# A complex linear-attention chunk rewritten: scores from two 64-row products per head, a block-diagonal state, no regrouping copies, hardware scans, and one subtraction on GpSimd

## The chip, the cores and the metric

The kernel runs on one core of a Trainium2 chip, with its five engines (TensorE, here PE; VectorE, DVE; ScalarE, ACT; GpSimd, POOL; SyncE, SP). The metric is the device time of one execution in microseconds; the kernel before takes 1257.93 us (median of three runs, 1257.11 to 1259.96). The profile and its rows are of one further execution of 1253.42 us.

## The reference, cut to what matters

Three layers follow each other. The first is a complex linear recurrence for each of 4 x 8 heads with 48 values per head and 768 steps; the other two are a dense layer with an ELU and a top-2 mixture of 8 experts:

```
S_re, S_im = ar*S_re - ai*S_im + outer(k[t], v[t]),  ar*S_im + ai*S_re      # per head, 48 x 48
y[t] = q[t] @ S_re                                                          # only the real part is read
x = y as rows [3072, 384]
g = elu(x @ w_in);  x = g @ w_out                                           # 384 -> 2048 -> 384
logits = x @ w_gate + log1p(exp(x @ w_noise)) * noise;  top 2 of 8 experts
out += weight * (relu(x @ w1[e]) @ w2[e])                                   # 384 -> 1024 -> 384
```

In (ar, ai) each step's factor is scaled so that its size is at most 0.999. All inputs are float32, except w_in and w_out, which come as float64 and are decoded on the chip.

## The kernel before

The recurrence is computed in chunks of 128 steps. A unit u is one chunk of two of the four batches; there are 12 units, and within a unit the batch index i is 0 or 1. Heads are taken in pairs p (four pairs per batch); a pair fills 128 partitions with 64 each, of which 48 are used (the rest are padding). For every unit the kernel makes the running product of the factors' sizes (tile `E`), its angle as cosine and sine (tile `X`, index 0 and 1), and from them the scaled keys `KK` and queries `X`, each with a cosine part and a sine part. The score of query t and key s of one head is the sum over 48 channels of cos-part times cos-part plus sin-part times sin-part.

In the kernel before, TensorE computes this sum as one product over 128 rows per head: 64 rows hold the cosine part and 64 the sine part of the same head. What DVE computes stands otherwise, with the two heads of a pair in the two halves of the partitions, so `by_head` (lines 678 to 684) regroups it, with three copies of 64x512 for the keys and three for the queries of each (u, i): 144 copies in all. The state `St` also stands by pair, and `diag` (L770) regroups it into one tile `Sc` per i with four copies of 48x192. In `y` (lines 787 to 805) a head's output is the query times `Sc` plus the masked scores `P` times `v`; the 128 tokens are split into two halves of 64 columns of the array (`halves`).

`m_pieces` makes the running product in `E` with steps over strided slices: seven of 128x128 elements (L633), four of 128x64 (L639), and one of 128x840 (L644) per unit.

The dense layer takes the 256 tokens of one unit in eight steps s (`f_pieces`): `l1` multiplies into `ph`, ACT and DVE form the ELU in `ge`, ACT rounds it to the high part `gh` (L859), DVE subtracts to get the low part `gl` (L860), and `l2` of the step two later multiplies both into `y`. `ge`, `gh` and `gl` have two buffers each. `r_pieces` picks the experts and POOL writes their tables by indirect DMA (L967). The expert layer runs at the end, when all units are done, from about 760 us on.

The order of work on each engine is not that of the code: `arrange` collects all instructions, gives each a cost, groups some into runs that stay together, and lists them by priority and by when their inputs should be ready; the engines then work each through its own list in order. PSUM is held in two rings of two banks for the attention: the rings' string gives `sc0`, `sc1`, `upd` and `y` one ring, the transposes and angles the other.

Of the kernel before, what the change touches and what calls it, by code (L numbers as in the profile page):

```python
# [27 lines left out]
def arrange(tc):  # L28
# [58 lines left out]
    def cost(n):  # L87
        i, k, c = ins[n], kinds[n], cells[n]
        if eng[n] == "PE":
            if k != "Matmult":  # L90
                return 20, 20
            mv = i.ins[0]
            dt = str(mv.dtype)
            cols = math.prod(x[1] for x in mv.bass_ap.ap[1:])
            if "32r" in dt:
                return (8 + .4385 * cols if cols > 128 else 110), 170 + .4385 * cols
            if "bf" in dt:
                return 26, 166
            if i.is_transpose:
                return 110, 273  # L100
            if i.tile_size[1] != 128 or i.tile_size[0] != 128:
                return 72, 229
            return (223, 387) if cols <= 128 else (1.72 * cols, 1.72 * cols + 170)
# [11 lines left out]
        if eng[n] == "DVE":  # L115
            if k == "Memset":
                return 30 + c * .8, 60 + c * .8
            if k == "Reciprocal":
                return 60 + c * 6, 150 + c * 6
            r = 1.042  # L120
            if k == "TensorCopy" or k == "TensorScalarPtr" and sum(x[4] == 0 for x in acc[n]) == 1:
                if not psum_in[n]:
                    r = .53
            if k == "TensorTensor" and c <= 128 and any(getattr(o, "bass_ap", None) is not None and len(o.bass_ap.ap) > 1 and o.bass_ap.ap[-1][0] > 1 and o.bass_ap.ap[-1][1] > 1 for o in i.outs):
                r = 1.9
            s = 58 + c * r + (60 if k == "TensorScalarPtr" and scal[n] else 0)
            return s, s + 92
# [4 lines left out]
        if k == "Memset":  # L132
            return 100 + c * .55, 100 + c * .55
        return 25, 25
# [5 lines left out]
    for n, i in enumerate(ins):  # L140
        e = eng[n]
        p = prev.get(e)
        if e == "PE" and p is not None and kinds[n] == kinds[p] == "Matmult":
            a, b = acc[p][0], acc[n][0]
            same = a[0] == b[0]
# [49 lines left out]
    for key, ts in tag.items():  # L195
        ts.sort(key=lambda t: users[t][0])
        nb = tiles[ts[0]].bufs or tiles[ts[0]].tag_meta.bufs
        for k, t in enumerate(ts):
# [3 lines left out]
            if k and nb > 1:  # L202
                p = users[ts[k - 1]]
                mine = set(p)
                roots = [x for x in p if not (deps[x] & mine)]
# [145 lines left out]
def tile_kernel(ctx, tc, q, k, v, a_re, a_im, w_in, w_out, w_gate, w_noise, noise, w1, w2, qp, kp, vp, ap,  # L351
# [73 lines left out]
    Sc = []  # L425
    for b in range(NB):
        s = wa.tile([128, HP, 2, D], F32, name=f"Sc{b}", bufs=1)
        nc.gpsimd.memset(s, 0.0)
        Sc.append(s)
# [182 lines left out]
    def m_pieces(u):  # L612

        P = []
        R = 8
        NK = L // R

# [12 lines left out]
        def cm1(t):  # L630
            def f():
                x = ET[u].rearrange("p q (k r) -> p (q k) r", r=R)
                tt(x[:, :, t], x[:, :, t], x[:, :, t - 1], op=OP.mult)  # L633
            return f

        def cm2(h):
            def f():
                x = ET[u].rearrange("p q (a b r) -> p (q a) b r", r=R, b=2 * h)[:, :, :, R - 1]
                tt(x[:, :, h:], x[:, :, h:], x[:, :, h - 1:h].to_broadcast([128, NP * NK // (2 * h), h]), op=OP.mult)  # L639
            return f  # L640

        def cm3():
            x = ET[u].rearrange("p q (k r) -> p q k r", r=R)
            tt(x[:, :, 1:, :R - 1], x[:, :, 1:, :R - 1],  # L644
               x[:, :, :NK - 1, R - 1:R].to_broadcast([128, NP, NK - 1, R - 1]), op=OP.mult)
            nc.vector.tensor_reduce(guard[:, u, :, 3], ET[u][:, :, L - 1].rearrange("p (i h) -> p i h", i=NB),
                                    axis=AX.X, op=OP.min)
        for t in range(1, R):
            P.append((0.2, cm1(t)))
        h = 1  # L650
        while h < NK:
            P.append((0.2, cm2(h)))
            h *= 2
        P.append((1.0, cm3))
        return P

    def a_pieces(u):
# [20 lines left out]
        def by_head(x, t):  # L678


            copy = nc.vector.tensor_copy
            copy(t[:64], x[64:, 0])
            copy(x[64:, 0], x[:64, 1])
            copy(x[:64, 1], t[:64])

        def kk(i):
            def f():
# [5 lines left out]
                by_head(k, nat["k", u, i])  # L693
            return f

        def qq(i):
            def f():
# [4 lines left out]
                by_head(x[:, :, o], b[:, o])  # L702
# [10 lines left out]
    def b_pieces(u):  # L713
# [18 lines left out]
        def upd(i):  # L732
            def f():
# [3 lines left out]
                for p in range(HP):  # L737
                    for x in range(2):
                        for j in range(2):
                            mm(pu[64 * j:64 * j + 64, p, x, :], kts[j][:, p, 64 * x:64 * x + 64],  # L740
# [25 lines left out]
        def diag(i):  # L766
            def f():
                for j in range(2):
                    for x in range(2):
                        nc.vector.tensor_copy(Sc[i][64 * x:64 * x + D, :, j, :],  # L770
                                              St[bat(u, i)][64 * j:64 * j + D, :, x, :])
            return f

        def sc(i):
            def f():
                ps = [psa.tile([128, HP, L], F32, name=f"sc{j}", **ring(f"sc{j}")) for j in range(2)]
                for p in range(HP):
                    for j in range(2):
                        mm(ps[j][:, p, :], KK[u, i][:, j, p, :], X[u][:, j, i * HP + p, :],  # L779
                           start=True, stop=True)  # L780
# [6 lines left out]
        def y(i):  # L787
            def f():
                b = bat(u, i)
                py = psa.tile([128, Dm], F32, name="py", **ring("y"))  # L790
                for p in range(HP):
                    for j in range(2):
                        h = 2 * p + j
                        oh = slice(h * D, (h + 1) * D)
                        halves = [slice(z * (L // 2), (z + 1) * (L // 2)) for z in range(2)]
                        if c:
                            for z in halves:
                                mm(py[z, oh], X[u][:, j, i * HP + p, z], Sc[i][:, p, j, :], start=True, stop=False,
                                   skip_group_check=True)
# [36 lines left out]
    def f_pieces(u):  # L836
# [4 lines left out]
        def l1(s):  # L841
            def f():
# [9 lines left out]
                with sooner(PAR.get("fs", 0.0)):  # L852
# [7 lines left out]
                    tt(gl, e, gh.bitcast(F32), op=OP.subtract)  # L860
# [718 lines left out]
```

## Time and profile before

| | |
|---|---|
| median of the runs | 1257.93 us |
| profiled execution, its span | 1253.42 us, 1251.6 us |
| PE busy | 1160.8 us, 93% of the span |
| DVE busy | 786.7 us, 63% |
| ACT busy | 648.9 us, 52% |
| POOL busy | 234.4 us, 19% |
| TensorE's granted clock, mean | 0.972 |

Busy shares are means over the whole span; the stages differ. Up to about 136 us the dense layer's weights are decoded beside the first units of attention; from there to about 760 us attention and dense layer run interleaved; after that come the experts. A matmul's row carries a duration with its latency, and matmuls overlap, so the distance from one start to the next says what a matmul takes of PE.

### The profile page before, as it was taken

How to read it: one execution, taken by the hardware profiler on the slowest of the kernel's cores; microseconds unless marked ns; L12 is line 12 of the kernel's file. 1: busy time of each engine (PE TensorE's matmuls, PEld its weight loads, DVE VectorE, ACT ScalarE, POOL GpSimd, SP SyncE). 2: the span in 40 equal slices, each digit the busy share in tenths (PEclk: the TensorE clock that was granted, in tenths of full speed). 3: DMA queues.
4: the chain of work that ended last, by engine and by line, in shares of the span. 5: the costliest groups of instructions: out<-in, count | busy, mean ns of one | idle time of the engine just before them, and what ended most of it. 6: DMA issues, size and time to landing. Idle time of an engine off the chain costs nothing.

```text
span 1251.6 us, 22832 instructions
## 1 busy us (share of the span) xinstructions
PE 1160.8 (93%) x8821; PEld 1070.9 (86%) x8821; DVE 786.7 (63%) x1782; ACT 648.9 (52%) x1299; POOL 234.4 (19%) x265
## 2 busy tenths in 40 slices
PE   4786998999999999899999999799999999999997
PEld 2464988888998999899999898789898989898996
DVE  5798998987987979697863556344434343443322
ACT  6877876768776777576554464332323232332111
POOL 2111000002002000200200302432424242424222
PEclk9697999999999999899999999999999999999999
DMA  6345520220220202120100133343424242423111
GB/s 218 118 160 179 182 81 24 72 94 12 84 75 21 81 22 79 18 92 31 30 11 28 52 103 119 109 127 96 134 90 136 83 137 85 131 85 108 36 45 34
DMA packets 64309, 107.05 MB, mean 86 GB/s; under 512 B 19967, under 2 KB 46310, under 8 KB 64192
## 3 DMA queue, kind: packets, MB, share of 16 engines
q1 hardware_dynamic: 50096, 65.65, 16.9%
q0 software_dynamic: 14096, 39.86, 10.2%
q8 instruction: 71, 1.16, 0.4%
q14 instruction: 46, 0.38, 0.1%
HBM read 86.98 MB, written 20.70 MB: 86 GB/s over the span
## 4 chain that ended last, share of the span: by engine, by line
PE 51%; DVE 25%; issue 14%; ACT 6%; DMA 2%; POOL 2%; POOLq 0%; SPq 0%; DVEq 0%; ACTq 0%
PE mpo L1096 18%; PE mph L1074 17%; PE ph L850 4%; PE y L874 4%; DVE gl L860 2%; DVE ge L856 2%; DVE E L633 2%; DVE X L701 2%; PE mtp L1059 1%; DVE P L783 1%; DVE KK L692 1%; DVE Sc L770 1%; PE sc L779 1%; ACT L577 1%; POOL table L967 1%
## 5 line engine op out<-in xcount | busy, mean ns | idle before, releaser
L1076 ACT ACTIVATE egh<-mph 128x320 fp32r<-128x320 f32 (+1 forms) x128 | 66.3, 518 | 233.9 <-PE mpo L1096 141.7
L967 POOL DMA_INDIRECT table<-route x48 | 47.1, 981 | 593.4 <-DVE route L961 275.4
L1096 PE MATMUL mpo<-weh,egh 128*128 128x384 f32 (+1 forms) x448 | 151.6, 338 | 0.0
L1096 PE MATMUL mpo<-weh,egl 128*128 128x384 f32 (+1 forms) x448 | 151.6, 338 | 0.0
L1096 PE MATMUL mpo<-wel,egh 128*128 128x384 f32 (+1 forms) x448 | 151.2, 337 | 0.0
L874 PE MATMUL y<-woh,gh 128*128 128x400 f32 x384 | 138.9, 362 | 0.0
L1101 DVE SCALAR_TENSOR_TENSOR ac<-mpo,slots,ac 128x384 f32<-128x384 f32 (+1 forms) x49 | 30.2, 617 | 171.5 <-PE mpo L1096 171.5
L874 PE MATMUL y<-woh,gl 128*128 128x400 f32 x384 | 133.0, 346 | 3.1 <-DVE gl L860 3.1
L874 PE MATMUL y<-wol,gh 128*128 128x400 f32 x384 | 131.5, 342 | 0.0
L1077 DVE SCALAR_TENSOR_TENSOR egl<-mph,egh 128x320 fp32r<-128x320 f32 (+1 forms) x128 | 75.1, 587 | 80.2 <-ACT egh L1076 80.2
L850 PE MATMUL ph<-xh,wih 128*128 128x256 f32 x576 | 106.4, 294 | 8.1 <-DVE ge L856 8.1
L1027 ACT ACTIVATE weh<-raw 128x384 fp32r<-128x384 f32 x128 | 65.3, 522 | 84.2 <-PE mpo L1096 60.0
L850 PE MATMUL ph<-xl,wih 128*128 128x256 f32 x576 | 101.5, 285 | 0.0
L850 PE MATMUL ph<-xh,wil 128*128 128x256 f32 x576 | 101.4, 285 | 0.0
L1104 POOL DMA_INDIRECT out_dram<-ac,slots x56 | 55.2, 987 | 239.4 <-DVE ac L1101 216.4
L850 PEld LDWEIGHTS ph<-xh,wih 128*128 128x128 f32 x576 | 88.4, 193 | 12.0 <-DVE ge L856 7.5
L854 ACT ACTIVATE ge<-ph 128x512 f32<-128x512 f32 x96 | 57.2, 596 | 63.5 <-DVE gl L860 39.7
L859 ACT ACTIVATE gh<-ge 128x512 fp32r<-128x512 f32 x96 | 60.1, 628 | 54.8 <-PE y L874 51.8
L860 DVE TENSOR_TENSOR gl<-ge,gh 128x512 fp32r<-128x512 f32 x96 | 66.2, 690 | 34.9 <-ACT gh L859 34.2
L856 DVE SCALAR_TENSOR_TENSOR ge<-ge,ph 128x512 f32<-128x512 f32 x96 | 65.5, 683 | 33.6 <-ACT ge L855 32.3
L1028 DVE TENSOR_TENSOR wel<-raw,weh 128x384 fp32r<-128x384 f32 x128 | 69.3, 555 | 23.9 <-ACT weh L1027 22.1
L850 PEld LDWEIGHTS ph<-xh,wil 128*128 128x128 f32 x576 | 83.8, 193 | 0.0
(207 smaller groups left out, 2831.9 us busy)
## 6 DMA issues: line engine op xcount, KB each, us to landing
raw<-in_moe_w_dram SPq DMA_DIRECT2D x128, 192.0 KB, 2.6
nat_a<-in_a_rows_dram SPq DMA_DIRECT2D x24, 512.0 KB, 3.6
raw<-in_moe_w_in_dram POOLq DMA_DIRECT2D x16, 384.0 KB, 3.7
raw<-in_moe_w_out_dram POOLq DMA_DIRECT2D x16, 384.0 KB, 3.5
q<-in_q_pairs_dram SPq DMA_DIRECT2D x24, 256.0 KB, 3.7
k<-in_k_pairs_dram SPq DMA_DIRECT2D x24, 256.0 KB, 2.8
vt<-in_v_rows_dram SPq DMA_DIRECT2D x24, 192.0 KB, 2.7
out_dram<-zero SPq DMA_DIRECT2D x24, 192.0 KB, 4.5
```

The costliest lines, as they stand in the source:

```text
L850: mm(ph[:, j, :], w[:, z, :], x[:, z, :], start=n == 0, stop=n == 3 * KD - 1)
L856: stt(e, e, -1.0, ph, op0=OP.add, op1=OP.max)
L859: act(gh, e, AF.Copy)
L860: tt(gl, e, gh.bitcast(F32), op=OP.subtract)
L874: mm(d["y"][i], g[:, j, i * L:(i + 1) * L], w, start=s == 0 and j == 0 and n == 0, stop=s == NS - 1 and j == 1 and n == 2)
L967: st = nc.gpsimd.indirect_dma_start(out=table[:, :], out_offset=bass.IndirectOffsetOnAxis(ap=idx, axis=0), in_=row, in_offset=None)
L1027: act(w[0], raw, AF.Copy)
L1028: tt(w[1], raw, w[0].bitcast(F32), op=OP.subtract)
L1074: mm(ph[:, :n], w[:, z, :], x[:, z, :], start=k == 0, stop=k == 3 * KD - 1)
L1076: act(gs[0][:, f, :n], ph[:, :n], AF.Relu)
L1077: stt(gs[1][:, f, :n], ph[:, :n], 0.0, gs[0][:, f, :n].bitcast(F32), op0=OP.max, op1=OP.subtract)
L1096: mm(po[:m], x[:, f, o:o + m], w, start=k == 0, stop=k == 3 * FE - 1)
```

## The change

Six edits, all in the first two stages:

- The scores of a head are two products of 64 rows each (cosine part, then sine part) that add up in the same PSUM bank. The two heads of a pair use the two halves of the array's rows, alternately. `by_head` and its 144 copies are gone.
- The state is one tile `Sc` for both i, with the two heads of a pair block-diagonal: 128 rows by 96 columns for each pair and part. `diag` is two copies of 64x384. A product of query and state covers both heads: 96 columns instead of 48, and as many instructions as before.
- The update `upd` takes keys from the cosine or sine transpose instead of from the head's.
- The running product is a scan instruction for each of the 8 pairs of a unit (128x128), instead of 12 strided multiplications.
- `gl` is computed by GpSimd instead of DVE.
- The planner has costs for the new instructions, keeps matmuls of 64 rows together as one run, and ties a buffer's next tile to the first root of the previous one instead of all.

```diff
@@ arrange
+            if i.tile_size[1] == 128 and i.tile_size[0] == 64:
+                return 117, 330
...
+            if getattr(i, "is_tensor_tensor_scan", False):
+                return 58 + c * 2.084, 150 + c * 2.084
...
-            same = a[0] == b[0]
+            same = a[0] == b[0] or tuple(i.tile_size) == tuple(ins[p].tile_size) == (64, 128) and not i.is_transpose
...
-                roots = [x for x in p if not (deps[x] & mine)]
+                roots = [next(x for x in p if not (deps[x] & mine))]
@@ tile_kernel
+    Sc = wa.tile([128, HP, 2, 2 * D], F32, name="Sc", bufs=1)
+    nc.gpsimd.memset(Sc, 0.0)
@@ m_pieces
+        def cum(q):
+            def f():
+                x = ET[u][:, q]
+                nc.vector.tensor_tensor_scan(x, x, ones, 1.0, op0=OP.mult, op1=OP.mult)
+            return f
...
+        for q in range(NP):
+            P.append((0.4, cum(q)))
+        P.append((0.1, least))
@@ a_pieces
-                by_head(k, nat["k", u, i])
...
-                by_head(x[:, :, o], b[:, o])
@@ b_pieces
-                            mm(pu[64 * j:64 * j + 64, p, x, :], kts[j][:, p, 64 * x:64 * x + 64],
+                            mm(pu[64 * j:64 * j + 64, p, x, :], kts[x][:, p, 64 * j:64 * j + 64],
...
-                    for x in range(2):
-                        nc.vector.tensor_copy(Sc[i][64 * x:64 * x + D, :, j, :],
-                                              St[bat(u, i)][64 * j:64 * j + D, :, x, :])
+                    nc.vector.tensor_copy(Sc[64 * j:64 * j + 64, :, :, j * D:(j + 1) * D],
+                                          St[bat(u, i)][64 * j:64 * j + 64])
...
-                    for j in range(2):
-                        mm(ps[j][:, p, :], KK[u, i][:, j, p, :], X[u][:, j, i * HP + p, :],
-                           start=True, stop=True)
+                    for x in range(2):
+                        for j in range(2):
+                            h = slice(64 * j, 64 * j + 64)
+                            mm(ps[j][:, p, :], KK[u, i][h, x, p, :], X[u][h, x, i * HP + p, :],
+                               start=x == 0, stop=x == 1, skip_group_check=True)
...
+                    if c:
+                        for x in range(2):
+                            for z in halves:
+                                mm(py[z, 2 * p * D:(2 * p + 2) * D], X[u][:, x, i * HP + p, z], Sc[:, p, x, :],
+                                   start=x == 0, stop=False, skip_group_check=True)
@@ f_pieces
-                    tt(gl, e, gh.bitcast(F32), op=OP.subtract)
+                    nc.gpsimd.tensor_tensor(gl, e, gh.bitcast(F32), op=OP.subtract)
```

The order of instructions moves with it. On PE, this is one unit's scores and the start of its outputs before, in the middle of the program (`sc_5438` and `sc_5439` are the two heads' banks of one batch, numbers are buffers):

```order
L779 MATMUL sc_5438<-X,KK 128x128
L602 MATMUL tp<-tri,nat_a 128x128 x4
L779 MATMUL sc_5438<-X,KK 128x128 x3
L602 MATMUL tp<-tri,nat_a 128x128 x4
L779 MATMUL sc_5439<-X,KK 128x128 x4
L850 MATMUL ph<-xh,wih 128x256 x3
L850 MATMUL ph<-xl,wih 128x256 x3
L850 MATMUL ph<-xh,wil 128x256 x3
L624 MATMUL tp<-ident,nat_a 128x128 x4
L798 MATMUL py<-Sc_109,X 64x48 x2
L801 MATMUL py<-vt,P 64x48 x2
L798 MATMUL py<-Sc_109,X 64x48 x2
```

And this is the same place in the changed kernel, from the end of such a run of scores, of which two rows stand here:

```order
L759 MATMUL sc_4697<-X,KK 128x128
L759 MATMUL sc_4698<-X,KK 128x128
L626 MATMUL tp<-ident,nat_a 128x128 x8
L855 MATMUL y_3152<-woh,gh 128x400
L855 MATMUL y_3152<-wol,gh 128x400
L855 MATMUL y_3152<-woh,gl 128x400
L705 MATMUL tp<-ident,KK 128x128 x8
L855 MATMUL y_3153<-woh,gh 128x400
L855 MATMUL y_3153<-wol,gh 128x400
L855 MATMUL y_3153<-woh,gl 128x400
L776 MATMUL py<-Sc,X 64x96 x4
L782 MATMUL py<-vt,P 64x48 x4
```

The scores of a (u, i) were eight products, one bank after the other and split around other work; they are now 16 products that alternate between the two banks, in one piece. Over the whole program the pieces of PE's list in which the array is split into smaller tiles go from 43 to 64: 24 of them are the scores, and the outputs and updates make 40.

On DVE, this is a stretch from a middle unit before, where keys and queries of one batch are scaled and regrouped:

```order
L682 COPY k<-KK 64x512
L700 TENSOR_TENSOR E<-E,q 128x512
L683 COPY KK<-KK 64x512
L701 TENSOR_TENSOR X<-X,E 128x2x512
L860 TENSOR_TENSOR gl<-ge,gh 128x512 x2
L817 TENSOR_TENSOR xl<-tp,xh 128x3x128
L682 COPY E<-X 64x512
L684 COPY KK<-k 64x512
L683 COPY X<-X 64x512
L856 SCALAR_TENSOR_TENSOR ge<-ge,ph 128x512 x2
L817 TENSOR_TENSOR xl<-tp,xh 128x3x128
L684 COPY X<-E 64x512
```

And a stretch with the same steps of a middle unit in the changed kernel (the list prints the scans of L635 under another name):

```order
L672 TENSOR_TENSOR KK<-KK,k 128x512
L611 SCALAR_TENSOR_TENSOR X<-X,tp 128x512 x2
L673 TENSOR_TENSOR KK<-KK,X 128x1024
L763 TENSOR_TENSOR P<-sc_5397,causal 128x512
L763 TENSOR_TENSOR P<-sc_5398,causal 128x512
L739 TENSOR_TENSOR s_5060<-sx,al 128x384
L681 TENSOR_TENSOR X<-X,E 128x2x512
L635 SCALAR_TENSOR_TENSOR E<-E,ones 128x128 x4
L748 COPY Sc<-St_108 64x8x48 x2
L740 TENSOR_TENSOR sx<-sx,al 128x384
L635 SCALAR_TENSOR_TENSOR E<-E,ones 128x128
L741 TENSOR_TENSOR St_106<-sx,s_5060 128x4x48
```

## Rows read from the trace of the kernel before

**Rows 1.** Busy times by stretch; columns are named in the first line.

```profile
core 0: us, PE busy (x) PEld busy (x) DVE busy (x) ACT busy (x) POOL busy (x), PEclk, DMA share, GB/s
0.00:150.00 150.00, 108.22 (x681) 81.82 (x682) 123.00 (x281) 110.28 (x241) 22.14 (x46) 0.84 0.51 169
150.00:450.00 300.00, 280.21 (x2901) 266.35 (x2900) 267.15 (x630) 218.88 (x427) 16.22 (x16) 0.99 0.20 63
450.00:750.00 300.00, 285.92 (x2539) 276.81 (x2538) 204.40 (x474) 180.02 (x335) 31.40 (x38) 0.99 0.16 47
750.00:1251.00 501.00, 486.49 (x2707) 445.89 (x2705) 192.13 (x400) 139.72 (x300) 164.60 (x165) 0.99 0.32 98
```

**Rows 2.** Who PE waited for, 150 to 760 us: total us, times, longest.

```profile
PE ph L850 <- DVE ge L856: 8.1, 11, 2.1
PE pr L949 <- DVE route L944: 6.3, 3, 2.7
PE tp L602 <- ACT nat_a L581: 4.6, 2, 3.9
PE y L874 <- DVE gl L860: 3.1, 4, 0.9
PE mtp L1059 <- DMA xr<-xs,slots: 2.6, 2, 2.5
...
PE tp L815 <- DVE X L607: 0.2, 1, 0.2
```

**Rows 3.** Chain of waits, 150 to 450 us, shares of this stretch.

```profile
by line: issue 9.1%; PE y L874 7.6%; PE ph L850 7.1%; DVE gl L860 5.3%; DVE ge L856 4.9%; DVE E L633 4.3%; DVE Sc L770 3.4%; DVE X L701 3.3%; DVE P L783 3.0%; DVE KK L692 2.4%; ACT L577 2.1%; PE sc L779 2.0%; ACT X L578 1.8%; PE tp L602 1.7
```

**Rows 4.** DVE groups up to 760 us: busy us, mean ns, idle before.

```profile
L860 DVE TENSOR_TENSOR gl<-ge,gh 128x512 fp32r<-128x512 f32 x96 | 66.2, 690 | 34.9 <-ACT gh L859 34.2
L633 DVE TENSOR_TENSOR E<-E 128x128 f32<-128x128 f32 x84 | 34.3, 408 | 1.6 <-ACT E L625 1.1
L692 DVE TENSOR_TENSOR KK<-KK,X 128x1024 f32<-128x1024 f32 x24 | 29.2, 1219 | 25.3 <-ACT X L578 25.2
L770 DVE COPY Sc<-St 48x192 f32<-48x192 f32 x80 | 20.6, 258 | 1.3
L639 DVE TENSOR_TENSOR E<-E 128x64 f32<-128x64 f32 x48 | 13.5, 282 | 0.2
L644 DVE TENSOR_TENSOR E<-E 128x840 f32<-128x840 f32 x12 | 12.5, 1040 | 0.0
L683 DVE COPY KK<-KK 64x512 f32<-64x512 f32 x24 | 10.1, 421 | 0.7
L783 DVE TENSOR_TENSOR P<-sc,causal 128x512 f32<-128x512 f32 x48 | 32.8, 685 | 1.6 <-PE sc L779 1.6
```

**Rows 5.** PE in order of time: start us, us, then the instructions.

```profile
240.03 0.34 PE L874 MATMUL y<-wol,gh 128*128 128x400 f32 x1
240.21 0.34 PE L874 MATMUL y<-woh,gl 128*128 128x400 f32 x1
240.48 0.32 PE L798 MATMUL py<-Sc,X 128*64 128x48 f32 x4
...
242.27 0.29 PE L801 MATMUL py<-vt,P 128*64 128x48 f32 x4
242.48 0.45 PE L874 MATMUL y<-woh,gh 128*128 128x400 f32 x1
242.77 0.35 PE L874 MATMUL y<-wol,gh 128*128 128x400 f32 x1
...
268.08 1.16 PE L779 MATMUL sc<-X,KK 128*128 128x128 f32 x8 [0.94 <-DVE X L683]
268.99 0.43 PE L874 MATMUL y<-woh,gh 128*128 128x400 f32 x1
```

**Rows 6.** POOL and ACT: a memset's group, and who waited for gl.

```profile
L428 POOL MEMSET Sc<- 128x384 f32 x2 | 0.9, 437 | 0.0
  ACT ge L854: 39.7, 39
```

More of the change, by code (lines that the diff above doesn't have):

```diff
@@ L133, in cost @@
             return 100 + c * .55, 100 + c * .55
+        if k in ("TensorTensor", "TensorReduce"):
+            s = 160 + c * (2.1 if k == "TensorTensor" else 1.3)
+            return s, s + 40
         return 25, 25
@@ L424, in tile_kernel @@
         St.append(wa.tile([128, HP, 2, D], F32, name=f"St{b}", bufs=1))
[L425 to L429, printed above, removed]
+    Sc = wa.tile([128, HP, 2, 2 * D], F32, name="Sc", bufs=1)
+    nc.gpsimd.memset(Sc, 0.0)
     def bat(u, i):
@@ L614, in m_pieces @@
         P = []
-        R = 8
-        NK = L // R
         def size(i):
@@ L628, in m_pieces, with least @@
             P.append((0.5, size(i)))
-        def cm1(t):
+        def cum(q):
             def f():
-                x = ET[u].rearrange("p q (k r) -> p (q k) r", r=R)
-                tt(x[:, :, t], x[:, :, t], x[:, :, t - 1], op=OP.mult)
-            return f
[L636 to L645, printed above, removed]
+                x = ET[u][:, q]
+                nc.vector.tensor_tensor_scan(x, x, ones, 1.0, op0=OP.mult, op1=OP.mult)
+            return f
+        def least():
             nc.vector.tensor_reduce(guard[:, u, :, 3], ET[u][:, :, L - 1].rearrange("p (i h) -> p i h", i=NB),
                                     axis=AX.X, op=OP.min)
[L648 to L654, printed above, removed]
+        for q in range(NP):
+            P.append((0.4, cum(q)))
+        P.append((0.1, least))
         return P
@@ L676, in g1 @@
             return f
[L678 to L684, printed above, removed]
         def kk(i):
@@ L790, in f @@
                 py = psa.tile([128, Dm], F32, name="py", **ring("y"))
+                halves = [slice(z * (L // 2), (z + 1) * (L // 2)) for z in range(2)]
                 for p in range(HP):
+                    if c:
[3 more added lines that the diff above has]
+                                   start=x == 0, stop=False, skip_group_check=True)
                     for j in range(2):
@@ L794, in f @@
                         oh = slice(h * D, (h + 1) * D)
[L795 to L799, printed above, removed]
                         for z in halves:
```

## Prediction

> **What bounds the kernel now.** I read the busy times by stretch first [rows 1]. After 750 us the experts keep PE busy for 486.5 of 501 us, and no edit touches them: that stage only moves with its start. Everything is decided before. Up to 150 us PE works 108 us and DVE 123, with ACT close behind at 110: the weights' decoding and the first units keep DVE longest, and PE waits. From 150 to 750 us PE is busy 566 of 600 us, and DVE 267 of 300 us in the first half and 204 in the second. So two engines are nearly full there, and the question is which of them the other waits for.
>
> Who PE waited for says it [rows 2]: eleven rows from 8.1 down to 0.2 us, 33.6 us in all, and nine of them, 26.4 us, name DVE. That is no more than the idle 34 us of rows 1, so a change that only relieves DVE can give back about 34 us in this stretch and not more. The chain of waits for 150 to 450 us [rows 3] agrees: PE's two dense-layer lines lead it, but `gl` (5.3% of 300 us), `E` L633 (4.3%) and `Sc` (3.4%) stand on it with 39 us, all three lines that the change alters. That these 39 us lie on the chain doesn't make them a gain, since PE's own list is 93% full beside them.
>
> **What DVE loses.** Durations are from [rows 4]. Each of the six groups of regrouping copies has 24 instructions of 0.41 to 0.43 us (one group stands there); 144 of them are 60.5 us. `gl` is 96 x 0.690 = 66.2 us. The running products are 34.3 + 13.5 + 12.5 = 60.3 us; in their place come 96 scans. No scan is in the trace: at least 0.28 us (the 64-element multiplication, half as many elements), at most 0.69 us (a 512-element one). I take 0.41 us, the row with as many elements, so 39 us: 21 us less (33 less to 6 more). `Sc` is 80 x 0.258 = 20.6 us; 40 copies of 64x384 lie between 0.258 (192 elements) and 0.421 (512), by proportion 0.36, so 14 us: 6 less. Together 60.5 + 66.2 + 21 + 6 = 154 of the 594.6 us that DVE works before 750 us [rows 1].
>
> **What POOL gains.** `gl` on POOL is not in the trace. A memset of 384 elements takes 0.437 us [rows 6], 0.58 us for 512; an instruction that reads two operands and writes one moves three times as much, 1.75 us. I take 1.2 us, halfway: 96 x 1.2 = 115 us over some 600 us, on an engine that is busy 48 us between 150 and 750. So POOL has room. A unit's eight `gl` take 10 to 14 us of some 50. A longer `gl` keeps the `ge` buffer longer, and ACT already waited 39.7 us for that [rows 6]; but two buffers cover two steps of PE's work, so this costs me nothing, and at most 0.5 us x 39 times, 20 us of ACT time, if ACT had no slack (it is busy 219 of 300 us at its fullest). The Trainium skill, GPSIMD Engine Reference, section 3.1, states about 2.6 cycles per element at 1.2 GHz for two inputs, an estimate of 1.1 us for 512 elements; no run here shows it, and the sum would be the same by it.
>
> **What PE gains.** Durations by start to start [rows 5].
> - Scores: eight instructions from 268.08 to 268.99 us, 114 ns each, 384 of them (two per product). Now there are 768 over half the rows, two heads alternating. If the halves work side by side, a pair takes 114 ns, and nothing is added; one after the other it is 384 x 114 ns = +44 us. The trace shows no such pair by rows, but by columns: 15 groups of four `py` instructions take 242.27 - 240.48 = 1.79 us, 30 ns each, where 48 columns at the scores' pace need 114 x 48/128 = 43 ns. They overlap, so I take zero.
> - State product: 640 instructions, 320 pairs of 60 ns now. With 96 columns a pair takes 114 x 96/128 = 85 ns if it overlaps: +25 ns x 320 = +8.0 us (nothing, if the 60 ns are a floor that hides the columns; +36 us if the two don't overlap).
> - Smaller tiles: the order has 64 stretches of them in place of 43. Going in costs 0.09 us (240.21 to 240.48, where `y` has 0.18), coming out 0.09 (242.27 to 242.48, where four take 0.12), and the first `y` after it 0.11 more: 0.29 x 21 = +6.1 us.
> That is 14.1 us more, in a stretch where PE is the fuller engine.
>
> **What comes back.** With 154 of 594.6 us gone, DVE falls from about 80% to under 60% of the time before 750 us; its queue seldom holds PE any more. I take 80% of the 33.6 us: not only the DVE rows, since ACT's inputs come from DVE too, and not all, since the wait for ACT's sine stays (DVE itself stood 25.2 us before `KK` for it, rows 4) and is what is late next. That is -26.9 us. Before the first `ge` DVE's list loses 18 of the copies, 7.6 us, and pays about 3 us for state work and an `X` that now stand earlier; 24 multiplications of 10.1 us become 24 scans of 9.8. That start gains 5 us (0 to 15: the idle 42 us of PE there mostly belong to the decoding, which stays). One `Sc` for both batches adds a wait: the second batch's two copies come after the first's state products on PE, and behind them in DVE's list stand the next `P` and `E`; with DVE under 60% full I count that as nothing, and 20 x 0.36 us = 7 us if it isn't hidden.
>
> Sum against the profiled execution: 1253.4 + 14.1 - 26.9 - 5 = 1235.6 us. The median of the runs is 4.5 us above that execution, so I forecast **1240 us**.
>
> **Rivals.**
> - *More comes back.* All 33.6 us go and the start gives 15: 14.1 - 33.6 - 15 = -34.5, so 1223 us, and 1209 if the 14.1 us on PE cost nothing. For it: DVE's three changed lines on the chain. Against it: PE is full beside them.
> - *POOL's `gl` holds DVE (the other side).* If DVE's instructions with two inputs in SBUF must wait while GpSimd reads, each `gl` can cost DVE its own 1.2 us: 115 of the 154 us are eaten. What comes back shrinks to a quarter, 8 of 32 us, against 14.1: slower by 6, 1264 us. It decides from about 0.9 us of delay per `gl` (86 us; the 68 left are 44% of 154, and 44% of 32 is the 14.1 that PE adds). For it: the two-input rows are most of what DVE keeps. Against it: DVE also has PSUM operands (`P`, `ge`) that could fill those times, and no row of this trace has POOL reading operands. The Trainium skill, SBUF — State Buffer, section Who interferes with whom, states just this: a DVE instruction with two SBUF inputs contends with a GpSimd instruction that reads SBUF, and the second to start is blocked to the end of the first. By that rule the time would be between 1250 and 1264 us; no run here shows it yet.
> - *The 64-row halves don't overlap.* +44 us on PE: 1284 us. Against it: the column halves do.
> - *The two scores' banks.* The alternating run needs both banks of its ring before its first product, where the first head's eight used to start with one. Each of the 24 runs can wait a masked multiplication longer (0.685 us, rows 4): 24 x 0.685 = 16 us, so 1256 us. For it: `upd`, `y` and both scores share two banks. Against it: PE's list has dense-layer work ahead of it.
>
> **How the numbers follow.** Forecast 0.48 (its own range 1228 to 1251: the start and the share that comes back), more comes back 0.17, POOL holds DVE 0.13, banks 0.14, halves one after another 0.08. About 0.2%, 2.5 us, is what a measurement can tell from no change. Faster than that is nearly all of the first (0.46), the second (0.17), and of the third and fourth the milder half (0.04 and 0.07): 0.74. Within it 0.08, from the edges of those two. Slower 0.18: the last (0.08) and the rest. The range from 1212 to 1264 us leaves out the halves (0.08) and the lowest edge of the second case.
>
> **What would show it.** In the profile after: no `KK`, `X` copies on DVE; DVE under 200 us in each 300 us before 750; PE's waits on DVE under 10 us; scores at 57 ns from start to start (114 would show the last-but-one rival), the state product at 42 to 45; DVE rows such as `KK` at 1.22 us as now (longer, with POOL at work, would show the lock); the experts' stretch as long as before and 15 to 20 us earlier. The forecast fails if PE's idle time stays near 34 us although DVE is relieved, or if DVE's remaining instructions grow.

## The result and the profile after

The changed kernel takes 1240.87 us (median of four runs, 1239.47 to 1243.75) against 1257.52 us for the kernel before beside it (four runs, 1255.99 to 1259.96): a ratio of 0.987, 95% interval 0.986 to 0.989. The forecast was 1240 us. The profiled execution took 1239.85 us with a span of 1238.1 us, 13.5 us less than before. In the experiments below the kernel before has medians from 1250.6 to 1257.2 us in three other sessions, so kernels of different sessions are compared by their ratios to it alone. A ratio does not settle everything: 1257.2 and 1250.6 us come from one chip, 0.5% apart, while the experts' stretch of kernels profiled beside them has one length (495.6 and 495.8 us from the last `y` on). So a difference between two sessions is uncertain by some 0.5%, about 7 us, beyond its interval. The planner alone, POOL's additional work, the scans twice and the old roots were measured in the session with 1250.6 us; where it matters, the difference of the times themselves stands beside that of the ratios.

First the busy times by stretch of the changed kernel; they answer to [rows 1], with the same columns (DVE is the third engine, POOL the fifth; PEclk stands behind the engines).

```profile
core 0: us, PE busy (x) PEld busy (x) DVE busy (x) ACT busy (x) POOL busy (x), PEclk, DMA share, GB/s
0.00:150.00 150.00, 110.93 (x848) 87.59 (x848) 124.29 (x280) 119.71 (x259) 24.79 (x47) 0.89 0.56 179
150.00:450.00 300.00, 288.02 (x3064) 274.10 (x3065) 205.74 (x435) 218.34 (x422) 77.02 (x59) 1.00 0.19 59
450.00:750.00 300.00, 291.67 (x2660) 280.08 (x2659) 169.34 (x392) 176.73 (x346) 101.83 (x90) 0.99 0.19 56
750.00:1238.00 488.00, 473.59 (x2637) 434.51 (x2635) 179.22 (x349) 128.62 (x275) 166.61 (x165) 0.99 0.31 94
```

DVE lost 96 us between 150 and 750 us, POOL gained 131, and PE's idle time there went from 33.9 to 20.3 us. The view of who PE waited for, 150 to 760 us, answers to [rows 2] (total us, times, longest).

```profile
PE pr L930 <- DVE route L925: 4.4, 4, 1.6
PE ph L831 <- DVE ge L837: 3.0, 3, 1.0
PE tp L606 <- ACT nat_a L585: 2.6, 2, 1.7
PE mtp L1040 <- DMA xr<-xs,slots: 2.6, 1, 2.6
PE sc L759 <- DVE X L681: 2.3, 3, 1.4
...
PE y L855 <- POOL gl L841: 0.9, 1, 0.9
```

All rows of this view add up to 21.2 us (33.6 before), those on DVE to 15.1 (26.4). No single row stands out any more. The chain of waits for 150 to 450 us, which answers to [rows 3], is now led by PE's own two dense-layer lines with 39%, where they had 14.7%:

```profile
by line: PE y L855 19.9%; PE ph L831 19.1%; issue 5.8%; PE sc L759 4.8%; PE py L776 3.9%; POOL table L948 3.2%; PE pu L719 2.4%; PE py L782 2.4%; DVE KK L673 2.3%; DVE X L681 2.3%; POOL gl L841 2.2%; DVE E L635 2.2%; PE tp L705 1.9%; DVE P 
```

The groups of DVE and POOL up to 760 us (busy us, mean ns, idle before) answer to [rows 4]:

```profile
L635 DVE TENSOR_TENSOR_SCAN E<-E,ones 128x128 f32<-128x128 f32 x96 | 39.7, 451 | 2.3 <-ACT E L627 2.1
L673 DVE TENSOR_TENSOR KK<-KK,X 128x1024 f32<-128x1024 f32 x24 | 30.3, 1265 | 42.7 <-ACT X L582 42.7
L748 DVE COPY Sc<-St 64x384 f32<-64x384 f32 x40 | 13.9, 348 | 0.3
L763 DVE TENSOR_TENSOR P<-sc,causal 128x512 f32<-128x512 f32 x48 | 31.4, 678 | 2.0 <-PE sc L759 2.0
L841 POOL TENSOR_TENSOR gl<-ge,gh 128x512 fp32r<-128x512 f32 x96 | 129.6, 1353 | 428.6 <-ACT gh L840 331.6 <-DVE nat_a L565 29.2 <-ACT lg L866 15.4
```

And PE in order of time (start us, us, then the instructions), which answers to [rows 5]:

```profile
301.88 0.55 PE L776 MATMUL py<-Sc,X 128*64 128x96 f32 x8
302.26 0.39 PE L782 MATMUL py<-vt,P 128*64 128x48 f32 x8
302.47 0.52 PE L776 MATMUL py<-Sc,X 128*64 128x96 f32 x8
302.82 0.39 PE L782 MATMUL py<-vt,P 128*64 128x48 f32 x8
...
310.24 2.14 PE L759 MATMUL sc<-X,KK 64*128 64x128 f32 x32
312.32 0.62 PE L831 MATMUL ph<-xh,wih 128*128 128x256 f32 x3
```

A run of 32 score instructions takes 312.32 - 310.24 = 2.08 us from its start to the next; inside a run two of them start every 112 ns (median), as one did before (114). Eight instructions of the state product take about 0.35 us from start to start (302.82 - 302.47), and the median of a pair is 83 ns.

Where the time came from, with the stretches cut at the first `ph` and at the last `y`: the first `ph` starts 4.6 us earlier (131.5 to 126.9 us); from there to the last `y` PE is idle 12.9 us less (33.9 to 20.9) and busy 2.5 us more (591.6 to 594.2); the experts' stretch is 1.5 us longer. Together -4.6 - 12.9 + 2.5 + 1.5 = -13.5 us.

There is a second thing in these stretches that the forecast did not look at, the granted clock. In the kernel before, 30 us at a time, it stands at 0.94 from 210 to 240 us, 0.94 from 390 to 420, 0.93 and 0.96 from 480 to 540; after, once at 0.94 (690 to 720), and 1.00 in all others between 150 and 750 us. Here is the first of these places in the kernel before, by PE in order of time:

```profile
215.17 3.36 PE L602 MATMUL tp<-tri,nat_a 128*128 128x128 f32 x16 [3.94 <-ACT nat_a L581]
218.19 0.68 PE L874 MATMUL y<-woh,gh 128*128 128x400 f32 x1
218.67 0.54 PE L874 MATMUL y<-wol,gh 128*128 128x400 f32 x1
```

and by busy time and clock, with the columns as above:

```profile
214.00:216.00 2.00, 0.83 (x6) 0.83 (x7) 1.79 (x3) 1.98 (x3) 0.00 (x0) 0.92 0.00 0
216.00:218.00 2.00, 2.00 (x11) 2.00 (x11) 1.94 (x4) 1.43 (x3) 0.00 (x0) 0.50 0.09 35
218.00:220.00 2.00, 2.00 (x11) 1.99 (x11) 1.97 (x3) 0.00 (x0) 0.00 (x0) 0.73 0.61 194
```

PE had waited 3.94 us for ACT, and then worked at half of its 2.4 GHz for some 3 us: a `y` product takes 0.54 to 0.68 us where it has 0.34. The other two places follow waits of 2.44 and 2.68 us for `route`. Lost at the lower clock, by (1 - granted clock) x 30 us, are 0.06, 0.06, 0.07 and 0.04 of 30 us = 6.9 us before, and 1.8 us after, there behind a wait of 2.57 us for a DMA. So about 5 us of what came back is clock that the longest waits had cost on top of themselves, and it hides a good part of what the change adds on PE. Not every long wait costs clock: behind this one in the kernel before, the clock stayed at 1.00.

```profile
715.11 0.55 PE L1059 MATMUL mtp<-ident,xr 128*128 128x128 f32 x3 [2.45 <-DMA xr<-xs,slots]
```

The experts' 1.5 us are clock too. PE's idle time there is the same (15.1 us in both), but apart from the last 5 us the clock falls to half for 3.4 us once in the kernel before, at 799 us, and twice in the changed one, at 776 and 786 us, which is 1.7 us more. The first of these two:

```profile
776.00:778.00 2.00, 2.00 (x8) 2.00 (x8) 0.84 (x2) 0.49 (x1) 1.44 (x2) 0.50 0.27 98
```

### The profile page after: what moved, and what is told of

It is laid out like the page before. It is cut to its first block, busy times and chain, and to the rows that moved or that the text cites. A ratio compares the mean times of both kernels' runs of the same rounds, so it can differ in the third digit from the quotient of the medians.

```text
span 1238.1 us, 23439 instructions
## 1 busy us (share of the span) xinstructions
PE 1164.2 (94%) x9205; PEld 1076.3 (87%) x9205; DVE 678.6 (55%) x1454; ACT 643.4 (52%) x1299; POOL 370.3 (30%) x360
## 4 chain that ended last, share of the span: by engine, by line
PE 68%; issue 11%; DVE 9%; ACT 5%; POOL 4%; DMA 2%; POOLq 0%; SPq 0%; DVEq 0%; ACTq 0%
PE mpo L1077 18%; PE mph L1055 17%; PE y L855 12%; PE ph L831 11%; PE sc L759 2%; PE py L776 2%; POOL table L948 2%; PE mtp L1040 1%; POOL gl L841 1%; PE py L782 1%; PE pu L719 1%; POOL raw L487 1%; PE tp L606 1%; DMA xr<-xs,slots 1%; ACT ge L835 1%
## 5 line engine op out<-in xcount | busy, mean ns | idle before, releaser
L841 POOL TENSOR_TENSOR gl<-ge,gh 128x512 fp32r<-128x512 f32 x96 | 129.6, 1353 | 428.6 <-ACT gh L840 331.6
L831 PE MATMUL ph<-xh,wih 128*128 128x256 f32 x576 | 103.2, 288 | 3.0 <-DVE ge L837 3.0
L1009 DVE TENSOR_TENSOR wel<-raw,weh 128x384 fp32r<-128x384 f32 x128 | 73.0, 586 | 30.4 <-ACT weh L1008 23.5
L1077 PEld LDWEIGHTS mpo<-wel,egh 128*128 128x128 f32 (+1 forms) x448 | 81.3, 182 | 2.9
L1077 PEld LDWEIGHTS mpo<-weh,egl 128*128 128x128 f32 (+1 forms) x448 | 81.2, 181 | 2.7
```

The costliest lines, as they stand in the source:

```text
L831: mm(ph[:, j, :], w[:, z, :], x[:, z, :], start=n == 0, stop=n == 3 * KD - 1)
L841: nc.gpsimd.tensor_tensor(gl, e, gh.bitcast(F32), op=OP.subtract)
L1009: tt(w[1], raw, w[0].bitcast(F32), op=OP.subtract)
L1077: mm(po[:m], x[:, f, o:o + m], w, start=k == 0, stop=k == 3 * FE - 1)
```

## The experiments

Ratios are to the kernel before, with 95% intervals. After itself is 0.987.

**The subtraction back on DVE, with the order made for that.**

```diff
-                    nc.gpsimd.tensor_tensor(gl, e, gh.bitcast(F32), op=OP.subtract)
+                    tt(gl, e, gh.bitcast(F32), op=OP.subtract)
```

> The changed kernel with gl subtracted on DVE again; the rest stays. Theory A (what DVE is relieved of comes back in proportion, 31 us for 154 us): 66 us return to DVE, so 13 us of the gain go, 1254 us. Rival B (PE is the bound, GpSimd's part brings nothing): 1241 us, within 3. Rival C (GpSimd's gl holds DVE's two-input instructions, and costs more than it relieves): under 1237 us.

Measured: 1233.64 us, ratio 0.982 (0.980 to 0.984). It is faster than after with the 66 us of `gl` back on DVE, whose busy time grows by 30 us only (679 to 709 over the whole span). The step "POOL's `gl` costs nothing" falls, and with it the idea that every microsecond taken from DVE comes back in part.

**The parts apart.** The strided multiplications in place of the scans (as in the kernel before, L633 to L644), all else as after:

```diff
-                nc.vector.tensor_tensor_scan(x, x, ones, 1.0, op0=OP.mult, op1=OP.mult)
+                tt(x[:, :, t], x[:, :, t], x[:, :, t - 1], op=OP.mult)
...
-        for q in range(NP):
-            P.append((0.4, cum(q)))
+        for t in range(1, R):
+            P.append((0.2, cm1(t)))
```

> The changed kernel with the running product made by strided multiplications again instead of scans. Theory A: 21 us return to DVE, 4 us of the gain go, 1245 us. Rival B (DVE has room now): 1241 us, within 2. Rival C (the gain sits in this shorter chain at each unit's start): 1250 us or more.

Measured: 1255.21 us, 1.000 (0.998 to 1.001).

The old scores, copies, update and the two old `Sc` tiles, with the scans, `gl` on POOL and the new planner:

```diff
+                by_head(k, nat["k", u, i])
...
+                by_head(x[:, :, o], b[:, o])
...
-                               start=x == 0, stop=x == 1, skip_group_check=True)
+                        mm(ps[j][:, p, :], KK[u, i][:, j, p, :], X[u][:, j, i * HP + p, :],
```

> Scans and GpSimd's gl alone: scores over 128 rows, regrouping copies and one state tile per batch as before. Theory A: 87 of 154 us are still off DVE, 17 of 31 us come back, and PE's 14 us of extra work are absent, so about 1240 us: the new scores would bring nothing of their own. Rival (the regrouping copies stand between the exponentials and the scores, and their going is the gain): 1252 us or more.

Measured: 1256.21 us, 1.001 (0.999 to 1.002).

The new scores and state alone (the edits of the first two kernels together):

```diff
-                nc.vector.tensor_tensor_scan(x, x, ones, 1.0, op0=OP.mult, op1=OP.mult)
+                tt(x[:, :, t], x[:, :, t], x[:, :, t - 1], op=OP.mult)
...
-                    nc.gpsimd.tensor_tensor(gl, e, gh.bitcast(F32), op=OP.subtract)
+                    tt(gl, e, gh.bitcast(F32), op=OP.subtract)
```

> The new scores, block-diagonal state and no copies alone; running products by multiplications and gl on DVE as before. Theory A: 67 us off DVE return 13 us, PE pays 14, so 1257 us, as before. Rival (the copies' going is the gain): 1245 us or less.

Measured: 1246.60 us, 0.993 (0.991 to 0.995).

And the kernel before with nothing but the planner's costs and its two new rules:

```diff
-            same = a[0] == b[0]
+            same = a[0] == b[0] or tuple(i.tile_size) == tuple(ins[p].tile_size) == (64, 128) and not i.is_transpose
...
-                roots = [x for x in p if not (deps[x] & mine)]
+                roots = [next(x for x in p if not (deps[x] & mine))]
```

> The kernel before with the changed planner. Its costs for scans, 64-row tiles and GpSimd have nothing to act on there, only the roots' rule has. If the gain is the kernel's own: 1256 us, within 3. If the roots' rule gives part of it: under 1252 us.

Measured: 1259.46 us, 1.007 (1.006 to 1.009).

These make a ladder: the planner alone +0.7%, then the new scores, state and missing copies -1.4% (1.007 to 0.993, 18 us; two sessions, and 13 us by the times themselves), then the scans -1.1% (to 0.982, 14 us), then `gl` on POOL +0.5% (to 0.987, 6 us). The other pairs agree: without scans `gl` on POOL costs 0.65% (0.993 to 1.000), and with the old scores the scans and POOL's `gl` together bring 0.7% (1.007 to 1.001). So the edits that take 67 us of copies (`by_head` and `Sc`) from DVE bring 13 to 18 us, after what they add on PE, and the 20 us of the running products 14: not in proportion to DVE's time.

**The engine of `gl` in a fixed order.** The planner sees the engine and plans by it. Here it is told one engine, and the other one executes the instruction. Told DVE, run on POOL:

```diff
+    real = list(eng)
+    for n in range(N):
+        if kinds[n] == "TensorTensor" and any(x[4] and x[0].startswith("gl_") for x in acc[n]):
+            eng[n] = "DVE"
...
-            e, g = eng[z], groups.get(z)
+            e, g = real[z], groups.get(z)
```

> The planner is told that gl is DVE's, so that all engines' lists are those of the kernel with gl on DVE (1233.6 us), but gl runs on GpSimd. Theory D (the seven microseconds that gl on GpSimd costs are the machine's: 1.35 us in place of 0.69, and DVE's instructions held meanwhile): 1240 us or more. Theory E (they are the order's, which the planner made for GpSimd): 1234 us, or less since DVE has 66 us less to do.

Measured: 1263.17 us, 1.005 (1.003 to 1.006), 2.3% or 29 us above the same order with `gl` on DVE.

Told POOL, run on DVE:

```diff
+            eng[n] = "Pool"
...
-            e, g = eng[z], groups.get(z)
+            e, g = real[z], groups.get(z)
...
-                    nc.gpsimd.tensor_tensor(gl, e, gh.bitcast(F32), op=OP.subtract)
+                    tt(gl, e, gh.bitcast(F32), op=OP.subtract)
```

> The mirror image: the lists that the planner made for gl on GpSimd (1240.9 us), but gl runs on DVE. Theory D: 1234 us, as with gl on DVE in its own order. Theory E: 1241 us, or more since DVE has 66 us more to do in an order that doesn't allow for it.

Measured: **1228.30 us, 0.978** (0.976 to 0.980), the fastest of all, 1% or 12 us below after with the same order. PE is idle 11.9 us between 150 and 750 us:

```profile
150.00:450.00 300.00, 291.91 (x3095) 278.43 (x3096) 223.18 (x482) 221.69 (x428) 16.84 (x16) 1.00 0.19 59
450.00:750.00 300.00, 296.24 (x2692) 284.14 (x2692) 190.78 (x464) 178.59 (x346) 39.60 (x43) 1.00 0.20 58
```

Part of what POOL's `gl` costs is read from who waited for it, 125 to 790 us. With the order of after and `gl` on DVE:

```profile
ACT ge L839 <- DVE gl L845: 0.9, 2, 0.6
```

in the changed kernel:

```profile
ACT ge L835 <- POOL gl L841: 23.2, 12, 3.4
```

in the order made for DVE, with `gl` on DVE:

```profile
ACT ge L835 <- DVE gl L841: 23.7, 28, 2.7
```

and in that order with `gl` on POOL:

```profile
ACT ge L839 <- POOL gl L845: 66.4, 49, 5.3
PE y L859 <- POOL gl L845: 15.8, 8, 4.0
```

ACT waits for the `ge` buffer that `gl` still reads. In the one order it waits 22 us longer when `gl` goes to POOL and the time grows by 12 us, in the other 43 and 29. This wait can be compared within one order only: with `gl` on DVE in its own order it is as long as in the changed kernel, at 0.982. The longer instruction is only a part: on POOL, `gl` also stands in line behind the experts' tables, as POOL in order of time shows for the last of these kernels (the `gl` at 397.11 us follows six tables):

```profile
394.85 0.97 POOL L952 DMA_INDIRECT table<-route  x1 [0.30 <-issue]
396.13 0.97 POOL L952 DMA_INDIRECT table<-route  x1 [0.30 <-issue]
397.11 1.28 POOL L845 TENSOR_TENSOR gl<-ge,gh 128x512 fp32r<-128x512 f32 x1
```

By a sum over the traces, 15.0 of the 23.2 us in the changed kernel are waits for a `gl` with tables just ahead of it (under 0.4 us of idling between), and in the last of these kernels 26.5 of ACT's 66.4 us and 11.2 of PE's 15.8.

DVE has a part as well. In the order of after, PE's waits for DVE (150 to 760 us) are 8.9 us with `gl` on DVE and 15.1 with it on POOL. One row of the 8.9 is

```profile
PE pr L934 <- DVE route L929: 2.5, 4, 1.1
```

where the changed kernel has 4.4 us: in four units the router's `route<-lg` takes 1.3 us beside a `gl` in place of 0.17, and PE waits about half a microsecond longer each time.

**POOL at work without PE depending on it.** The kernel just called the fastest, and POOL subtracts the same operands once more into a scratch tile that nobody reads, in four pieces of 128 columns:

```diff
+                    gd = wf.tile([128, L], BF, name="gd", tag="gd", bufs=1)
+                    for j in range(2):
+                        for h in range(0, NT, L):
+                            nc.gpsimd.tensor_tensor(gd, e[:, j, h:h + L], gh[:, j, h:h + L].bitcast(F32), op=OP.subtract)
```

> The kernel of e6 (gl on DVE, 1228.3 us), and beside it GpSimd subtracts the same operands once more, in four pieces of 128 columns for each gl, into a scratch tile that nobody reads; the lists of the engines are almost those of e6. No wait for a result of GpSimd is added, only that it reads ge and gh (and so keeps ge a little longer). If gl on GpSimd costs 12.6 us because GpSimd's reading holds DVE: 1238 us or more. If because a gl of 1.35 us reaches PE and ACT later than one of 0.69: 1228 us, within 3.

Measured: 1279.45 us, 1.022 (1.020 to 1.023). This was to isolate what POOL's reading does to DVE, and it doesn't: the four pieces (0.60 us each in the mean) keep `ge` longer than one instruction does, and that is the wait which grew:

```profile
ACT ge L841 <- POOL gd L851: 70.1, 40, 4.1
```

What it does show: DVE's instructions up to 760 us are stretched in total as much as in the changed kernel (28 us in both, summed over the trace against each form's median with `gl` on DVE in the order of after), ACT waits three times as long, and the time is 3.5% more. What makes this kernel slower than the changed one is not the stretching.

**More work on DVE.** Each scan runs twice, the first time into a scratch tile (43 us more of DVE):

```diff
+                xd = wa.tile([128, L], BF, name="xd", tag="xd", bufs=1)
+                nc.vector.tensor_tensor_scan(xd, x, ones, 1.0, op0=OP.mult, op1=OP.mult)
```

> The changed kernel with every scan run twice, the first time into a scratch tile: 96 x 0.45 = 43 us more on DVE, in the planner's knowledge. Theory A (DVE's time counts in proportion, 0.2 us for each): 9 us, 1250 us. Theory F (only DVE's work before PE is filled counts, 24 scans or 11 us of it before the first step of the dense layer and as much in the first two units): 1250 to 1262 us. If the 14 us that the scans brought are not DVE's time but the order: 1241 us, within 3.

Measured: 1246.83 us, 0.996 (0.995 to 0.998). That is 0.9% or 12 us more than after, and 6 us by the times themselves: 0.14 to 0.27 us for each microsecond of DVE. The profiled executions are 9.3 us apart, and 5.7 of that is the start: the first `ph` comes at 132.6 us instead of 126.9.

**One half of the rows after the other.** All of a run's products of one head first, then the other's:

```diff
-                for p in range(HP):
-                    for x in range(2):
-                        for j in range(2):
+                for j in range(2):
+                    for p in range(HP):
+                        for x in range(2):
```

> The changed kernel with the scores of one head first and then of the other, so that neighbouring products use the same half of the rows. If alternating halves run side by side, as the prediction took it, the scores lose that here: 768 instructions at about 112 ns instead of 56, 43 us more of PE, and 1270 to 1284 us (PE's 20 us of idle time can take some of it). If the halves never overlapped, 1241 us.

Measured: 1271.85 us, 1.010 (1.008 to 1.012), 2.3% or 29 us above after. The run in the middle, in order of time:

```profile
313.33 3.50 PE L759 MATMUL sc<-X,KK 64*128 64x128 f32 x32
316.75 1.16 PE L606 MATMUL tp<-tri,nat_a 128*128 128x128 f32 x8
```

It takes 3.42 us instead of 2.08, and 24 x 1.34 = 32 us is near the 29 us of the difference in time: alternating halves work side by side, the same half twice does not.

**The planner's rules.** The costs stay, both rules go back:

```diff
-            same = a[0] == b[0] or tuple(i.tile_size) == tuple(ins[p].tile_size) == (64, 128) and not i.is_transpose
+            same = a[0] == b[0]
...
-                roots = [next(x for x in p if not (deps[x] & mine))]
+                roots = [x for x in p if not (deps[x] & mine)]
```

> The changed kernel with the planner's two rules as before (no runs across the two banks, all roots tied). If the edits to the kernel make the gain: 1241 us, within 3. If the planner's rules make it: 1250 us or more. Without the run the scores may be split in pieces, each with its own 0.3 us for the change of tiles: then 24 to 48 pieces more, 7 to 14 us.

Measured: 1340.71 us, 1.066 (1.065 to 1.068), the slowest of all. PE in order of time shows why:

```profile
461.95 0.49 PE L759 MATMUL sc<-X,KK 64*128 64x128 f32 x2
462.37 1.16 PE L606 MATMUL tp<-tri,nat_a 128*128 128x128 f32 x8
463.45 0.71 PE L759 MATMUL sc<-X,KK 64*128 64x128 f32 x4
464.09 1.16 PE L606 MATMUL tp<-tri,nat_a 128*128 128x128 f32 x8
```

The 32 score instructions come in pieces, mostly of two to six, and PE's list has 225 stretches of smaller tiles in place of 64. Two of the instructions take 0.42 us here and four 0.64, where they have 0.11 and 0.22 at 56 ns each. There are two costs in this. The two more in the piece of four take 0.22 us, 0.11 each, as in the run with one half after the other: inside a piece the halves no longer alternate. The other 0.42 - 0.22 = 0.2 us is each piece's own. Over the trace 96 score instructions start within 0.04 us of the one before, where the changed kernel has 370. So about 274 x 0.11 = 30 us are lost alternation, and 179 more pieces (203 for 24) at 0.2 us are 36: together the 66 us by which the scores' time on PE grows (51 to 117 us, from a piece's first start to the next instruction).

Only the rule of the roots as before, the run kept together:

> The changed kernel with only the rule on buffers' roots as before; the scores stay in one piece. If the 100 us of e8 are the scores in pieces (179 more stretches of small tiles, and heads that no longer alternate): 1241 us, within 6. If the roots' rule has part of it: more.

Measured: 1256.20 us, 1.005 (1.004 to 1.007). So this rule alone is worth 1.8% in the changed kernel (23 us, or 15 by the times themselves), and the other one the remaining 6.1% (77 us, or 85), which buys both, fewer pieces and halves that alternate. The view of who PE waited for shows two rows that were 4.4 and 3.0 us in the changed kernel:

```profile
PE pr L930 <- DVE route L925: 10.6, 5, 3.4
PE ph L831 <- DVE ge L837: 9.8, 10, 2.5
```

**Waits and time together.** The sum of PE's waits from 150 to 760 us, what the lower clock cost from 150 to 750 us, and the start of the first `ph`, for the kernels with the new scores in one alternating run, beside their ratios:

| kernel | PE's waits, us | lower clock, us | first `ph`, us | ratio |
|---|---|---|---|---|
| order of after, `gl` on DVE | 12.2 | 0 | 127.7 | 0.978 |
| `gl` on DVE | 13.2 | 3.4 | 125.9 | 0.982 |
| new scores alone | 18.0 | 3.4 | 129.0 | 0.993 |
| after | 21.2 | 1.7 | 126.9 | 0.987 |
| scans twice | 24.6 | 1.7 | 132.6 | 0.996 |
| products by steps | 25.0 | 5.1 | 136.2 | 1.000 |
| roots as before | 29.1 | 5.1 | 125.3 | 1.005 |
| order made for DVE, `gl` on POOL | 30.7 | 10.2 | 125.3 | 1.005 |
| POOL subtracts as well | 45.9 | 12.0 | 130.9 | 1.022 |

The time grows by more than the waits: from the first row to the last by 4.4%, 55 us, for 34 us of waits. Waits, clock and start together make between about half and nearly all of each row's distance from the first.

## Why the prediction came out right, and where it did not

The time was 1240.9 us for 1240, but as a sum whose errors cancel, which is luck. By its own steps:

| step | forecast, us | found |
|---|---|---|
| scores on PE | 0 | pairs of 112 ns instead of 114: 0 |
| state product | +8.0 | pairs of 83 ns for 60, 23 x 320 = +7.4 |
| 21 stretches of small tiles | +6.1 | a run of scores takes 1.99 us (median of 24), 0.2 more than its 16 pairs, and 0.09 on the way in: 24 x 0.29 = +7.0 |
| PE's waits | -26.9 | -12.9 from the first `ph` on |
| start | -5 | -4.6 |
| clock | not in it | about -5 between 150 and 750 us |
| experts' stretch | 0 | +1.5, by the clock |
| profiled execution to median | +4.5 | +1.0 |

- **What bounds the kernel** held: PE is the fuller engine before 750 us, its idle 34 us were all that DVE could give back, and 38% of them came.
- **PE's additions** held. By a sum over the trace from start to start, the state product takes 8.5 us more between the first `ph` and the last `y`, and the scores 5.0, which would be 6.8 if not three (u, i) instead of two had theirs before the first `ph` (96 of 768 instructions, where it was 32 of 384). PE's busy time grew by 2.5 us only, since the dense layer's two lines take 7.7 us less, some 5 of them by the clock, and the products of `P` 2.3 less; the forecast had neither.
- **What DVE loses** was right in each row: a scan has 0.41 us undisturbed (0.41 forecast), a copy of 64x384 348 ns (0.36), but DVE's busy time up to the last `y` fell by 108 us (600.9 to 493.1), not 154. The sum of its durations fell by 127 us (682 to 555): POOL stretches what stays by the 27 us between (below). And the durations of neighbours overlap, as these three rows of DVE in order of time show: 0.68 us each, but 0.60 from start to start. Over all instructions the overlap is 0.06 us each; with 327 fewer, that is 20 us that the sum of durations counted and the engine never spent.

```profile
156.55 0.68 DVE L763 TENSOR_TENSOR P<-sc,causal 128x512 f32<-128x512 f32 x1
157.15 0.68 DVE L837 SCALAR_TENSOR_TENSOR ge<-ge,ph 128x512 f32<-128x512 f32 x1
157.75 0.68 DVE L763 TENSOR_TENSOR P<-sc,causal 128x512 f32<-128x512 f32 x1
```

- **"What comes back" is the step that failed.** It took 80% of the waits, in the belief that DVE's total decides. 12.9 us came back, not 26.9. The ladder shows that a microsecond of DVE has no fixed price: 14 us for the 20 of the running products, 13 to 18 with the 67 of the copies, 6 to 12 for 43 added, and less than nothing for the 66 of `gl`.
- **"POOL's longer `gl` costs me nothing" failed too.** It took 1.2 us for an instruction that has 1.35, which is near, but it counted on two buffers of `ge` covering it. In the same order the move to POOL costs 12 us, and 29 us in the other. The bound that stood beside it, 20 us of ACT's time, is near the 22 us by which ACT's wait grows in the same order, but it was made of 39 waits of 0.5 us; the trace has 12 waits of up to 3.4 us, most of that time behind the experts' tables, which the forecast did not look at.
- **The planner's rules had no term at all.** The roots' rule is worth 15 to 23 us in the changed kernel, and the rule that keeps a run together some 80; in the kernel before both, with the new costs, make it 0.7% slower. Without the first of them the changed kernel would stand at 1.005 (0.999 by the times themselves), with nothing left of the gain.

Of the rivals, *more comes back* is what the same order gives with `gl` on DVE (0.978, 1230 us against the 1223 forecast). *The halves one after another* and *the banks* are out: alternating heads run side by side, and no row of PE's waits has the scores waiting for `P`. *POOL's `gl` holds DVE* is there, and smaller than the rival needed. One `KK`, which takes 1.22 us elsewhere, shows it in the order of time of all engines:

```profile
159.26 1.49 POOL L841 TENSOR_TENSOR gl<-ge,gh 128x512 fp32r<-128x512 f32 x1 [5.10 <-ACT gh L840]
...
159.55 2.29 DVE L673 TENSOR_TENSOR KK<-KK,X 128x1024 f32<-128x1024 f32 x1
```

`KK` starts 0.29 us behind `gl` and takes 1.07 us more, nearly what is left of `gl` (160.75 - 159.55 = 1.20). The Trainium skill, SBUF — State Buffer, section Who interferes with whom, states that a DVE instruction with two SBUF inputs contends with a GpSimd instruction that reads SBUF, and that the ports they share are an exclusive lock. The trace agrees, and gives the size: of `KK` the mean is 1.27 us, the scans take 451 ns in place of 408, and over all of DVE's instructions 27 us are added, 0.28 us for each `gl` where the rival needed 0.9. Instructions with an operand in PSUM are not stretched: `P` has 678 ns (685 before), `ge` 684.

Of the signs that the forecast named, the scores at 57 ns, the state product at 42 and the experts' 15 us earlier came; DVE stayed at 205.7 us in the first 300 where under 200 was said, and PE's waits on DVE at 15.1 us where under 10 was.

What stays open: how much of the 12 us that POOL's `gl` costs is the lock and how much the `ge` buffer, since the run that was to tell it held the buffer as well (the lock has about 2 us at the router, and PE's waits for DVE grow by 6 in all); why the scans bring 14 us for 20 of DVE, the shorter work or the other order; and how much a second `Sc` tile would bring, which was not tried.

## What to carry to other kernels

Price a move to another engine by the buffer that the slower instruction keeps and by the queue that it joins, not by the busy time it takes off: here taking 66 us of `gl` from DVE made the kernel 6 us slower, and 12 in the same order. Where a planner writes the order, vary its rules in both kernels, since its rules can be worth more than the edit (7.9% here), and compare engines with the order held fixed. When you forecast what a wait is worth, look at the granted clock behind it: the few longest waits cost PE a stretch at 1.2 GHz as well.

## What the runs showed of the hardware

- Behind waits of 2.4 to 3.9 us PE's clock was granted at half for some 3 to 7 us, in a stretch that has 1.00 otherwise; behind another wait, of 2.45 us, it stayed at 1.00.
- Two score products on opposite halves of the rows take 112 ns a pair, two on the same half 112 ns each, although in both cases the operands and the number of instructions are the same.
- A run of 64-row products between full ones took about 0.2 us more than its pairs, and 0.09 on the way in. Cut into 203 pieces instead of 24, the scores took 117 us of PE instead of 51, nearly half of the increase because products on one half stood next to each other.
- Some DVE instructions that started beside a GpSimd subtraction ended later by nearly what it had left to run: `KK` took 2.29 us instead of 1.22, `route<-lg` 1.3 instead of 0.17.
- A GpSimd subtraction of 512 columns takes 1.27 us at least, 1.35 in the mean and 3.03 at most, against 0.69 us on DVE; pieces of 128 columns (into bf16) take 0.60 us in the mean (0.47 in the median), so four of them take longer than one of 512.
